# Gated mix of cached attention and a GeGLU feed-forward block, decode step: TensorE's work of 31 tiles as a hardware loop, values in one buffer, keys in two, semaphores by hand

## The chip, the core and the metric

The kernel runs on one NeuronCore of a Trainium2 chip. The core has five engines that run their own instruction streams and meet at semaphores: TensorE (PE in the profile; its weight loads are listed apart as PEld), VectorE (DVE), ScalarE (ACT), GpSimd (POOL) and SyncE (SP). Here SP issues all transfers; they run on 16 DMA engines, which read device memory (HBM) and write the core's working memory, SBUF. Matrix products land in a second, smaller memory, PSUM. The metric is the device time of one execution in microseconds; the kernel before took 1314.42 us (median of three runs, 1314.0 to 1314.48).

## What is computed

```python
x = A_x                                                  # 4 x 1 x 512
g = sigmoid((x * gate_w).sum(-1, keepdims=True))
q = (x @ wq) -> 4 x 32 heads x 1 x 128
scores = einsum("bhqd,bhkd->bhqk", q, k_cache) * 128 ** -0.5     # 4096 keys per head
o = einsum("bhqk,bhkd->bhqd", softmax(scores), v_cache)
a = o -> 4 x 1 x 4096 @ wo
b = (gelu(x @ w_gate) * (x @ w_up)) @ w_down             # 512 -> 1792 -> 512
out = g * a + (1 - g) * b
```

Everything is float32. The two caches, 4 x 32 x 4096 x 128 each, are 268 MB apiece; the weights together are 27.8 MB. Each cache element is used once.

## The kernel before

The batch of 4 and the 32 heads are cut into NT = 32 tiles: tile i takes batch row b = i % 4 and four heads of group g = i // 4. The keys of a tile are one SBUF tile of 128 partitions x 16384 floats (8.39 MB, 64 KB to a partition): 32 partitions per head, each with R = 128 consecutive keys of 128 numbers. The values of a tile have the same layout.

SBUF has room for three such tiles (pool `kv`, three buffers in rotation). Every large load takes the next buffer, in the order in which SP issues it: wq, then keys and values of tile 0, keys and values of tile 1 and so on, before the last values the two feed-forward weights `w_gate` and `w_up` together, and after them `w_down` with 18 of wo's 32 rows per partition, and the remaining 14 rows in five pieces. `load_next` (L105) issues one load. A load into a buffer waits until the last reader of what lies there is done, so in the steady state values i+1 go where keys i lay, and keys i+2 where values i lay.

For a tile i the work is this:

- `multiply(i)` (L195): DVE multiplies the keys by the query, which `spread` has laid out for four batch rows at once in `QB`. The last RP = 20 of the 128 keys of each partition are multiplied into PSUM (`big`, L198), the first 108 in place in SBUF (L199).
- `add_up(i)` (L201): DVE sums the 108 products of SBUF (L202) and then the 20 of PSUM (L203) over the 128 numbers; this gives `SC`.
- `weights(i)` (L205): the largest score of each head (DVE, L208 to L212), then four exponentials with row sums on ACT (L215), one for each head, into `PM` and `RS`.
- `values(i)` (L224): 32 float32 matmuls with `PM` as weights and the values as moving operand, 512 columns each, into four column groups of one PSUM bank, `po`. Each is two passes in the profile, 64 records to a tile.
- `gather(i)` (L232): ACT copies `po` to `o`, a matmul with `wide` folds it into the rows of batch row b of `g`.
- Every fourth tile: `totals` (L220, sums over the partitions), `turn` (L240, turns the group's result), `divide` (L248, DVE, into `OT`) and `spread` (L184, the next group's queries).

The order is written out by hand in the loop of L281 to L300: `values(i-1)` and its gathering stand behind `multiply(i)`. Semaphores are put in by the framework. All instructions of all tiles stand one after another in each engine's stream.

In the last round `ffn_up` (L253) runs on PE before `add_up(31)`, and `gelu` on DVE and ACT after it. The tail from L304 projects the hidden layer and the attention output with `down`, turns `OT` into `OW`, adds wo's last rows as their pieces land (L342 to L350), and stores the result (L353).

## Time and profile before

| what | value |
|---|---|
| median of three runs | 1314.42 us |
| the profiled execution, its own time | 1313.86 us |
| the profiled execution, span on the core | 1312.1 us |
| DVE busy | 1141.9 us (87%) |
| PE busy | 381.7 us (29%) |
| ACT busy | 106.9 us (8%) |
| bytes moved by DMA | 565.07 MB, mean 431 GB/s |

The profile is one execution. Its span runs from the first to the last instruction on the core; the execution's own time has 1.76 us more around it. L12 is line 12 of the kernel before. A row of the groups gives busy time and mean duration, and behind the second bar the idle time of the engine just before these instructions, with what ended most of it. Rows of the timeline give the start in us, the duration, the engine, the line, the operation, and in brackets how long the engine had been idle and what released it; "SPq" is SP issuing a transfer. Rows of a window give the stretch in us, its length, the busy time of each engine with its instructions, the granted TensorE clock, the DMA engines' mean busy share and GB/s; packets count where they start, so that a share over a short stretch can exceed 1.

### The profile page before, as it was taken

How to read it: one execution, taken by the hardware profiler on the slowest of the kernel's cores; microseconds unless marked ns; L12 is line 12 of the kernel's file. 1: busy time of each engine (PE TensorE's matmuls, PEld its weight loads, DVE VectorE, ACT ScalarE, POOL GpSimd, SP SyncE). 2: the span in 40 equal slices, each digit the busy share in tenths (PEclk: the TensorE clock that was granted, in tenths of full speed). 3: DMA queues.
4: the chain of work that ended last, by engine and by line, in shares of the span. 5: the costliest groups of instructions: out<-in, count | busy, mean ns of one | idle time of the engine just before them, and what ended most of it. 6: DMA issues, size and time to landing. Idle time of an engine off the chain costs nothing.

```text
span 1312.1 us, 6178 instructions
## 1 busy us (share of the span) xinstructions
PE 381.7 (29%) x2590; PEld 99.6 (8%) x2590; DVE 1141.9 (87%) x280; ACT 106.9 (8%) x344; POOL 0.7 (0%) x6
## 2 busy tenths in 40 slices
PE   2132113333212233221333321233332123332147
PEld 0000001000000001000010000000010000100012
DVE  1788899988899988988989888998889898898891
ACT  0000010001000010000000001000110001000001
POOL 0000000000000000000000000000000000000000
PEclk9666566666566666656666656666665566666579
DMA  9999999999999999999999999999999999999998
GB/s 416 440 424 446 418 442 422 442 432 438 434 430 436 432 434 440 434 430 434 430 440 432 438 430 434 430 436 438 432 440 424 440 428 438 442 424 442 420 421 351
DMA packets 10863, 565.07 MB, mean 431 GB/s; under 512 B 1212, under 2 KB 1228, under 8 KB 1620
## 3 DMA queue, kind: packets, MB, share of 16 engines
q1 hardware_dynamic: 10836, 564.69, 99.5%
q8 instruction: 20, 0.33, 0.1%
q14 instruction: 7, 0.06, 0.0%
HBM read 564.67 MB, written 0.01 MB: 430 GB/s over the span
## 4 chain that ended last, share of the span: by engine, by line
DVE 42%; DMA 41%; PE 12%; ACT 3%; issue 2%; SPq 0%; DVEq 0%; ACTq 0%
DMA kv<-in_A_k_cache 38%; DVE SC L202 18%; DVE kv L199 18%; PE po L229 11%; DVE SC L203 3%; ACT PM L215 3%; DVE big L198 2%; DMA kv<-in_A_wo 2%; DMA o<-in_A_x 2%; DVE m L208 0%; PE po L168 0%; PE big L168 0%; PE sm L221 0%; DVE mt L210 0%; DVE nm L212 0%
## 5 line engine op out<-in xcount | busy, mean ns | idle before, releaser
L229 PE MATMUL po<-kv,PM 128*16 128x512 f32 x2048 | 293.7, 738 | 664.9 <-ACT PM L215 664.9
L202 DVE TENSOR_REDUCE SC<-kv 128x108 f32<-128x13824 f32 x32 | 465.7, 14553 | 3.2
L199 DVE TENSOR_TENSOR kv<-kv,QB 128x13824 f32<-128x13824 f32 x32 | 465.6, 14551 | 0.0
L198 DVE TENSOR_TENSOR big<-kv,QB 128x2560 f32<-128x2560 f32 x32 | 90.7, 2833 | 103.9 <-DMA kv<-in_A_k_cache 103.9
L215 ACT ACTIVATE PM<-SC,nm 32x128 f32<-32x128 f32 x128 | 65.9, 515 | 775.7 <-DVE nm L212 749.2
L229 PEld LDWEIGHTS po<-kv,PM 128*16 128x16 f32 x2048 | 61.8, 113 | 882.6 <-ACT PM L215 679.9
L203 DVE TENSOR_REDUCE SC<-big 128x20 f32<-128x2560 f32 x32 | 90.1, 2815 | 0.0
L221 PE MATMUL sm<-RS,ones 128*128 128x16 f32 x16 | 4.9, 385 | 200.7 <-ACT PM L215 200.7
L235 ACT ACTIVATE o<-po 128x512 f32<-128x512 f32 x32 | 19.1, 597 | 303.5 <-PE po L229 303.5
L238 PE MATMUL g<-o,wide 128*64 128x512 f32 x64 | 34.3, 618 | 24.3 <-ACT o L235 24.3
L215 ACT ACTIVATION_READ_ACCUMULATOR PM<-SC,nm 32x1 f32 x128 | 24.9, 195 | 0.0
L221 PEld LDWEIGHTS sm<-RS,ones 128*128 128x128 f32 x16 | 4.0, 311 | 202.8 <-ACT PM L215 202.8
L142 DVE COPY xT<-sm 128x32 f32<-128x32 f32 x4 | 0.5, 184 | 21.1 <-PE sm L140 21.1
L250 DVE RECIPROCAL ri<-sm 128x16 f32<-128x16 f32 x8 | 2.0, 249 | 10.0 <-PE sm L246 10.0
L238 PEld LDWEIGHTS g<-o,wide 128*64 128x64 f32 x64 | 6.1, 134 | 53.8 <-ACT o L235 53.8
L208 DVE TENSOR_REDUCE m<-SC 128x1 f32<-128x128 f32 x32 | 9.2, 286 | 1.1
L246 PE MATMUL sm<-ident,gs 64*128 64x16 f32 x64 | 8.5, 262 | 4.8 <-ACT gs L242 4.8
L178 DVE COPY QT<-big 128x16 f32<-128x16 f32 x8 | 0.9, 180 | 10.1 <-PE big L176 10.1
L352 DVE COPY res<-g 128x128 f32<-128x128 f32 x1 | 0.3, 292 | 10.5 <-PE g L349 10.5
L189 PE MATMUL po<-ident,QX 128*128 128x128 f32 x64 | 9.2, 286 | 0.0
L260 PE MATMUL po<-kv,xT 128*32 128x448 f32 x64 | 8.1, 661 | 3.5 <-DMA kv<-in_B_w_up 3.5
L190 ACT ACTIVATE QB<-po 128x512 f32<-128x512 f32 x8 | 4.8, 597 | 52.1 <-DVE kv L199 51.4
(65 smaller groups left out, 95.7 us busy)
## 6 DMA issues: line engine op xcount, KB each, us to landing
kv<-in_B_w_gate SPq DMA_DIRECT2D x1, 3584.0 KB
kv<-in_B_w_up SPq DMA_DIRECT2D x1, 3584.0 KB, 23.3
kv<-in_B_w_down SPq DMA_DIRECT2D x1, 3584.0 KB
kv<-in_A_wo SPq DMA_DIRECT2D x1, 2560.0 KB, 18.6
kv<-in_A_wo SPq DMA_DIRECT2D x1, 2048.0 KB, 23.0
kv<-in_A_wo SPq DMA_DIRECT2D x2, 1024.0 KB, 17.2
kv<-in_A_wo SPq DMA_DIRECT2D x1, 768.0 KB
kv<-in_A_k_cache SPq DMA_DIRECT2D x32, 30.5
```

The costliest lines, as they stand in the source:

```text
L189: nc.tensor.matmul(t[:, b, :], QX[:, b].rearrange("p h k -> p (h k)"), ident, start=True, stop=True)
L198: nc.vector.tensor_tensor(big, k[:, R1:], q.to_broadcast([P, RP, D]), op=OP.mult)
L199: nc.vector.tensor_tensor(k[:, :R1], k[:, :R1], q.to_broadcast([P, R1, D]), op=OP.mult)
L202: nc.vector.tensor_reduce(SC[:, :R1], keys(i)[:, :R1], axis=AX.X, op=OP.add)
L203: nc.vector.tensor_reduce(SC[:, R1:], big, axis=AX.X, op=OP.add)
L208: nc.vector.tensor_reduce(m1, SC, axis=AX.X, op=OP.max)
L215: nc.scalar.activation(PM[s, :, h], SC[s, :], AF.Exp, bias=nm[s, :], scale=1.0, accum_out=RS[s, b, h:h + 1])
L221: nc.tensor.matmul(tot.rearrange("p b h -> p (b h)"), ones, RS.rearrange("p b h -> p (b h)"), start=True, stop=True)
L229: nc.tensor.matmul(po[32 * c:32 * c + M], p[:, j * M:(j + 1) * M], T["v", i][:, j * RJ * D:(j + 1) * RJ * D], start=j < 4, stop=j >= n - 4)
L235: nc.scalar.activation(o, po, AF.Copy)
L238: nc.tensor.matmul(G[g], wide[:, (3 - b) * M:(7 - b) * M], o, start=b == 0, stop=b == B - 1)
L246: nc.tensor.matmul(quo, gs[:, j, :], pick[:, :, j, :], start=j == 0, stop=j == RJ - 1)
```

## The change

The whole kernel body stands in one critical section in which the framework adds no semaphores. `Line` keeps, for each engine, the number of marked instructions and what it has already waited for.

- Values always lie in one buffer, `V`; keys alternate between two, `K[0]` and `K[1]`. wq is loaded into `V` first, then keys 0 and 1; values 0 follow when PE is done with wq. In the loop SP issues keys i+2 when the scores of tile i are summed, then values i+1 when `values(i)` is done. So values i+1 stand behind keys i+2 in the queue, where before they stood ahead of them.
- DVE multiplies all 128 keys of a partition in place in one instruction and sums them in one; `big`, the PSUM tile of products, is gone.
- PE's work of tiles 0 to 30 is one hardware loop on PE alone (`nc.tensor.Fori`): the query of the next tile (one matmul instead of four every fourth tile), the totals, the 32 value matmuls, and the turning (four matmuls), now done for each tile. The gathering matmul and the copy of `g` are gone; DVE divides for each tile. Inside the loop PE waits on counters that it lowers again (`token_a`, `token_d`, `sem_v`).
- The feed-forward weights go into `K[0]` after the scores of tile 30 and ahead of values 31, `w_down` and the first of wo into `K[1]` after the scores of tile 31, the last of wo into `K[0]` after the hidden layer is done. Feed-forward work on PE follows the loop and comes ahead of tile 31's values.
- At the end SP issues the store, GpSimd clears the semaphores, and SP waits for the store.

```diff
+class Line:
+
+
+    def __init__(self, engine, sem):
+        self.engine, self.sem, self.n, self.seen = engine, sem, 0, {}
+
+    def do(self, instruction):
+        instruction.then_inc(self.sem, 1)
+        self.n += 1
+        return self.sem, self.n
+
+    def wait(self, *marks):
+        for sem, n in marks:
+            if self.seen.get(id(sem), 0) < n:
+                self.engine.wait_ge(sem, n)
+                self.seen[id(sem)] = n
...
+    K = [kv.tile([P, TW], F32, name=f"k{s}") for s in range(2)]
+    V = kv.tile([P, TW], F32, name="v")
...
-    T = {}
-
-    def place(key):
-        T[key] = kv.tile([P, TW], F32, name="kv")
-        return T[key]
...
-    def load_kv(kind, i):
-        nc.sync.dma_start(place((kind, i)), heads(kc if kind == "k" else vc, i))
...
-    for i in range(NT):
-        LOADS.append(lambda i=i: load_kv("k", i))
-        if i == NT - 1:
-            LOADS.append(load_ffn_up)
-        LOADS.append(lambda i=i: load_kv("v", i))
-    LOADS += [load_down, load_last]
-    LOADS = iter(LOADS)
-
...
+    def load(dst, src, sem=None, name=None):
+        sem = sem or semaphore(name)
+        nc.sync.dma_start(dst, src).then_inc(sem, 16)
+        return sem, 16
+
+    def load_k(i):
+        load(K[i % 2], heads(kc, i), sem_k[i % 2])
+
+    def load_v(i):
+        load(V, heads(vc, i), sem_v)
+
+    got_q = load(V, wq.rearrange("(p c) n -> p (c n)", c=KC), name="got_q")
+    x_sb = o[:B]
+    got_x = load(x_sb, x.rearrange("b s d -> (b s) d"), name="got_x")
+    gw = gs[:B]
+    got_g = load(gw, gate_w.rearrange("(o n) -> o n", o=1).to_broadcast([B, DM]), name="got_g")
+    load_k(0)
+    load_k(1)
...
-    def multiply(i):
-        k = keys(i)
-        q = QB[:, i % B, None, :]
-        nc.vector.tensor_tensor(big, k[:, R1:], q.to_broadcast([P, RP, D]), op=OP.mult)
-        nc.vector.tensor_tensor(k[:, :R1], k[:, :R1], q.to_broadcast([P, R1, D]), op=OP.mult)
-
-    def add_up(i):
-        nc.vector.tensor_reduce(SC[:, :R1], keys(i)[:, :R1], axis=AX.X, op=OP.add)
-        nc.vector.tensor_reduce(SC[:, R1:], big, axis=AX.X, op=OP.add)
...
+    def spread_query(i):
+        g, b = divmod(i, B)
+        return nc.scalar.activation(QX, QT[:, b, HT * g:HT * g + HT, None].to_broadcast([P, HT, PH]), AF.Copy)
+
+    def spread():
+        return nc.tensor.matmul(qp[:, :D], QX.rearrange("p h k -> p (h k)"), ident, start=True, stop=True)
+
+    def take_query(i):
+        return AC.do(nc.scalar.activation(QB[i % 2], qp[:, :D], AF.Copy, scale=scale))
+
+    def totals():
+        return nc.tensor.matmul(tot, ones, RS, start=True, stop=True)
+
+    def values():
         p = PM.rearrange("p r h -> p (r h)")
         n = R // RJ
         for j in range(n):
             c = j % 4
-            nc.tensor.matmul(po[32 * c:32 * c + M], p[:, j * M:(j + 1) * M],
-                             T["v", i][:, j * RJ * D:(j + 1) * RJ * D], start=j < 4, stop=j >= n - 4)
-
...
+    def turn():
+        for j in range(RJ):
+            t = nc.tensor.matmul(quo, o[:, j * D:(j + 1) * D], pick[:, j, :], start=j == 0, stop=j == RJ - 1)
...
+    at_spread = [(PE.sem, PE.n + 3 * i + 1) for i in range(L1)]
+    at_values = [(PE.sem, PE.n + 3 * i + 2) for i in range(L1)]
+    at_turn = [(PE.sem, PE.n + 3 * i + 3) for i in range(L1)]
+    with nc.tensor.Fori(0, L1):
+        spread().then_inc(PE.sem, 1)
+        nc.tensor.wait_ge(token_a, 2).then_inc(token_a, -2)
+        nc.tensor.wait_ge(token_d, 1).then_inc(token_d, -1)
+        totals()
+        nc.tensor.wait_ge(sem_v, 16).then_inc(sem_v, -16)
+        values().then_inc(PE.sem, 1)
+        nc.tensor.wait_ge(token_a, 1).then_inc(token_a, -1)
+        turn().then_inc(PE.sem, 1)
+    PE.n += 3 * L1
+
+    summed, have_nm, have_OT = {}, {}, {}
...
+    def keys(i):
+        k = K[i % 2].rearrange("p (r d) -> p r d", d=D)
+        DV.wait((sem_k[i % 2], 16 * (i // 2 + 1)), have_QB[i])
+        DV.wait(DV.do(nc.vector.tensor_tensor(k, k, QB[i % 2][:, None, :].to_broadcast([P, R, D]), op=OP.mult)))
+        sc = SC[i % 2]
+        summed[i] = DV.do(nc.vector.tensor_reduce(sc, k, axis=AX.X, op=OP.add))
+        DV.wait(summed[i])
+        DV.wait(DV.do(nc.vector.tensor_reduce(m1, sc, axis=AX.X, op=OP.max)))
+        DV.wait(DV.do(nc.vector.transpose(mt, m1.to_broadcast([P, 32]))))
+        have_nm[i] = DV.do(nc.vector.tensor_reduce(NM[i % 2], mt, axis=AX.X, op=OP.max, negate=True))
+
...
+    def divide(i, at):
         g, b = divmod(i, B)
...
+        DV.wait(at)
+        DV.wait(DV.do(nc.vector.reciprocal(ri, tot)))
+        return nc.vector.tensor_tensor(OT[:, b, HT * g:HT * g + HT], quo, ri, op=OP.mult)
...
+    def weights(i):
+        AC.wait(have_nm[i])
+        if i:
+            AC.wait(at_values[i - 1])
+        for h in range(HT):
+            s = slice(h * PH, (h + 1) * PH)
+            t = nc.scalar.activation(PM[s, :, h], SC[i % 2][s, :], AF.Exp, bias=NM[i % 2][s, :], scale=1.0,
+                                     accum_out=RS[s, h:h + 1])
+        return t
+
+    SP.wait(wq_done)
+    load_v(0)
+    for i in range(NT):
+        keys(i)
+        if i > 0:
+            divide(i - 1, at_turn[i - 1]).then_inc(token_d, 1)
+        if i < L1:
+            AC.wait(at_spread[i])
+            have_QB[i + 1] = take_query(i + 1)
+            if i + 2 < NT:
+                spread_query(i + 2).then_inc(token_a, 1)
+            else:
+                nc.scalar.sem_inc(token_a, 1)
+            weights(i).then_inc(token_a, 1)
+            AC.wait(at_values[i])
+            nc.scalar.activation(o, po, AF.Copy).then_inc(token_a, 1)
+        if i + 2 < NT:
+            SP.wait(summed[i])
+            load_k(i + 2)
+        if i + 1 < L1:
+            SP.wait(at_values[i])
+            load_v(i + 1)
+    have_PM = AC.do(weights(L1))
+
+    f, down = K[0], K[1]
+    wo_rows = wo.rearrange("(p i) n -> p (i n)", i=WR)
+    SP.wait(summed[NT - 2])
+    got_up = [load(f[:, s * KC * F:(s + 1) * KC * F], a.rearrange("(p c) n -> p (c n)", c=KC), name=f"got_up{s}")
+              for s, a in enumerate((w_gate, w_up))]
+    SP.wait(at_values[L1 - 1])
+    load_v(L1)
+    SP.wait(summed[L1])
+    got_down = load(down[:, :DR * DM], w_down.rearrange("(p i) n -> p (i n)", i=DR), name="got_down")
+    got_wo = [load(down[:, (DR + r0) * DM:(DR + r1) * DM], wo_rows[:, r0 * DM:r1 * DM], name=f"got_wo{r0}")
+              for r0, r1 in ((0, W0), (W0, W1))]
...
-    for i in range(NT):
-        g, b = divmod(i, B)
-        multiply(i)
-        if i > 0:
-            if b == 0:
-                totals(g - 1)
-            values(i - 1)
-            gather(i - 1)
-            load_next()
-        if b == 0 and i > 0:
-            turn(g - 1)
-        if b == B - 1 and i < NT - 1:
-            spread(g + 1)
...
+    SP.wait(have_hT)
+    got_w = []
+    r0 = 0
+    for n in PIECES:
+        got_w.append(load(f[:, r0 * DM:(r0 + n) * DM], wo_rows[:, (W1 + r0) * DM:(W1 + r0 + n) * DM],
+                          name=f"got_w{r0}"))
+        r0 += n
+
...
+    SP.wait(DV.do(nc.vector.tensor_copy(res, acc)))
+    load(out.rearrange("b s (c n) -> c (b s) n", c=4), res[::8], stored)
+    nc.sync.sem_inc(parting, 1)
+    nc.gpsimd.wait_ge(parting, 1).then_inc(parting, -1)
+    nc.gpsimd.sem_clear(range(counters[0].num, counters[-1].num + 1))
+    nc.sync.wait_ge(stored, 16).then_inc(stored, -16)
```

## The prediction, on record before the result

> **What bounds the kernel now.** I read the head of the page first, with the DMA queues.

> ```profile
> span 1312.1 us, 6178 instructions
> PE 381.7 (29%) x2590; PEld 99.6 (8%) x2590; DVE 1141.9 (87%) x280; ACT 106.9 (8%) x344; POOL 0.7 (0%) x6
> q1 hardware_dynamic: 10836, 564.69, 99.5%
> q8 instruction: 20, 0.33, 0.1%
> q14 instruction: 7, 0.06, 0.0%
> ```

> DVE at 87% looks like the busiest engine, but the data queue's packets fill 99.5% of 16 DMA engines' span. Every byte of caches and weights is still moved by the changed kernel, so the question is whether the transfers can be fed without holes, and what else uses the DMA engines. Next I cut the span into stretches (stretch, length, busy time of the engines, granted clock, DMA share, GB/s).

> ```profile
> 400.00:800.00 400.00, 110.05 (x706) 27.28 (x706) 365.41 (x76) 32.56 (x108) 0.00 (x0) 0.63 1.00 434
> 1200.00:1306.00 106.00, 51.28 (x416) 14.85 (x416) 77.39 (x33) 10.84 (x32) 0.00 (x0) 0.73 0.99 426
> 1275.00:1279.00 4.00, 0.00 (x0) 0.00 (x0) 3.93 (x4) 0.00 (x0) 0.00 (x0) 0.50 0.78 314
> ```

> The middle runs at a share of 1.00 and 434 GB/s: no hole to close. The last stage has one, 0.78 over 4 us, about 0.9 us for the average DMA engine. Then the timeline, for one tile, with its neighbours in the first and last tile.

> ```profile
> 42.30 2.83 DVE L198 TENSOR_TENSOR big<-kv,QB 128x2560 f32<-128x2560 f32 x1 [4.38 <-DMA kv<-in_A_k_cache]
> 80.81 2.83 DVE L198 TENSOR_TENSOR big<-kv,QB 128x2560 f32<-128x2560 f32 x1 [3.11 <-DMA kv<-in_A_k_cache]
> ...
> 622.27 9.30 PE L229 MATMUL po<-kv,PM 128*16 128x512 f32 x64 [26.92 <-ACT PM L215]
> 623.10 2.83 DVE L198 TENSOR_TENSOR big<-kv,QB 128x2560 f32<-128x2560 f32 x1 [3.13 <-DMA kv<-in_A_k_cache]
> 623.96 0.17 PEld L229 LDWEIGHTS po<-kv,PM 128*16 128x16 f32 x4 [0.68 <-issue]
> 624.81 0.17 PEld L229 LDWEIGHTS po<-kv,PM 128*16 128x16 f32 x4 [0.68 <-issue]
> 631.64 0.33 SPq L77 DMA_DIRECT2D kv<-in_A_k_cache  x1
> 655.08 0.33 SPq L77 DMA_DIRECT2D kv<-in_A_v_cache  x1
> 663.01 2.83 DVE L198 TENSOR_TENSOR big<-kv,QB 128x2560 f32<-128x2560 f32 x1 [4.44 <-DMA kv<-in_A_k_cache]
> ...
> 1243.90 2.83 DVE L198 TENSOR_TENSOR big<-kv,QB 128x2560 f32<-128x2560 f32 x1 [3.13 <-DMA kv<-in_A_k_cache]
> ```

> In all these rows DVE starts a tile when its keys land, after 3 to 4 us of idling: the transfers set the pace. From the first tile to the last, 31 tiles took 1243.90 - 42.30 = 1201.6 us, 38.76 each, and a tile's keys or values 19.38. The rows also give the lead, the time from a load's issue to the landing of the load ahead of it, when its own bytes can flow. Values issued at 655.08 follow keys that landed at 663.01: 7.9 us. Keys issued at 631.64 follow values that landed 19.4 after 623.1: 10.8 us. With these leads the share is 1.00.

> **The change part by part.** First DVE, by the groups (busy us, mean ns, idle before).

> ```profile
> L202 DVE TENSOR_REDUCE SC<-kv 128x108 f32<-128x13824 f32 x32 | 465.7, 14553 | 3.2
> L199 DVE TENSOR_TENSOR kv<-kv,QB 128x13824 f32<-128x13824 f32 x32 | 465.6, 14551 | 0.0
> L208 DVE TENSOR_REDUCE m<-SC 128x1 f32<-128x128 f32 x32 | 9.2, 286 | 1.1
> L250 DVE RECIPROCAL ri<-sm 128x16 f32<-128x16 f32 x8 | 2.0, 249 | 10.0 <-PE sm L246 10.0
> L251 DVE TENSOR_TENSOR OT<-sm,ri 128x16 f32<-128x16 f32 x8 | 1.4, 175 | 0.3
> ```

> Multiplying and summing all 16384 numbers in SBUF takes 14.55 x 16384 / 13824 = 17.25 us each, 34.5 together. Three small reductions, each at most L208's 0.29, and the division, now once a tile (0.25 + 0.18), add 1.3. That makes 35.8 us against 38.76 for the transfers. The 3.0 us between them cover it; DVE would have to lose all of them before the span grew. Dropping the products in PSUM is worth nothing by itself. It also takes away an early release: before, the key buffer was free after L202, ahead of the sums of `big`. Now it is free 34.5 us after the keys land.

> Keys i+2 may be issued then, and can flow when values i+1's predecessors are through: keys i land, values i, keys i+1 and values i+1 in the old order; now keys i, values i-1, keys i+1, values i, and then keys i+2. That is 3 x 19.38 = 58.1 us after keys i landed. The lead is 58.1 - 34.5 = 23.6 us, far over the 7.9 of before. Cost nothing; the price if the cover were gone is 1 us per tile and us.

> Values i+1 wait for `values(i)`, and this chain is the tighter one. Values i land, PE multiplies, SP issues. The rows from 622.27 to 631.64 show the same chain, 9.4 us. Its upper bound is a PE that stays slow: 0.85 us between the two loads of four weights at 623.96 and 624.81, and 16 such groups, 13.7 us. Values i+1 can flow after keys i+2, 19.38 after values i landed. The lead is 10.0 us, at worst 5.7. I take 10.0, since PE idles about as long ahead of it as before. That is again no shorter than the 7.9 that sufficed, so nothing.

> The query of keys i+2 now comes through PE's loop: values i land, 9.4 us of matmuls, a copy of `po`, four turning matmuls, the back edge, one `spread` matmul, a copy. The copies and matmuls have rows here:

> ```profile
> L235 ACT ACTIVATE o<-po 128x512 f32<-128x512 f32 x32 | 19.1, 597 | 303.5 <-PE po L229 303.5
> L246 PE MATMUL sm<-ident,gs 64*128 64x16 f32 x64 | 8.5, 262 | 4.8 <-ACT gs L242 4.8
> L238 PE MATMUL g<-o,wide 128*64 128x512 f32 x64 | 34.3, 618 | 24.3 <-ACT o L235 24.3
> L189 PE MATMUL po<-ident,QX 128*128 128x128 f32 x64 | 9.2, 286 | 0.0
> L221 PE MATMUL sm<-RS,ones 128*128 128x16 f32 x16 | 4.9, 385 | 200.7 <-ACT PM L215 200.7
> ```

> 0.6 for each copy, 2 x 0.3 for the two passes of `spread`, 8 x 0.26 for turning at most: 13.3 us, 6 us before keys i+2 land. A late query would delay only DVE, whose release of the buffer has 23.6 us to spare. On PE two gathering records per tile go, and turning, totals and spreading are done for every tile instead of every fourth; all of it lies in PE's idle time.

> Next the instruction fetch, which does lie on the bounding resource. 0.33 MB over PE's 5180 instructions is 64 bytes each, so q8 is PE's stream, in 20 pieces of 16 KB, 256 instructions. Its 0.1% of the span is 1.3 us on each of 16 engines, 0.7 to 2.0 by rounding. Of 2590 matmul records 2048 + 64 + 64 + 64 + 16 belong to tiles, and 334 stay. The loop body has 64 + 8 + 2 + 2 = 76 and stands once; tile 31 adds 74, the first query 2. That is 486, a fifth: 4 pieces for 20, if the loop's code is fetched once. 16/20 x 1.3 gives -1.05 us, between -0.5 and -1.6.

> The two ends:

> ```profile
> 0.74 0.39 SPq L110 DMA_DIRECT2D kv<-in_A_wq  x1
> ...
> 1261.11 4.91 PE L260 MATMUL po<-kv,xT 128*32 128x448 f32 x32 [3.52 <-DMA kv<-in_B_w_up]
> 1275.88 0.33 SPq L86 DMA_DIRECT2D kv<-in_B_w_down  x1
> 1286.26 21.62 DMA kv<-in_A_wo
> 1309.33 0.67 SPq L353 DMA_DIRECT2D out<-res  x1
> ```

> At the start keys 2 can be issued when tile 0 is summed, 42.30 + 34.5 = 76.9; values 0 take the place that keys 1 had in the queue, landing at 80.8. The lead is 3.9 us, the shortest of the changed kernel. Before, `w_down` had the like: issued at 1275.88, while the values ahead of it landed 19.4 after `w_up` (1261.1), at 1280.5: 4.6 us. That is the stretch at 0.78. Some of the 16 engines ran dry there while the last one, which sets a landing, was still at work. So 0 to 0.9 us; I take 0.2, as only the last engine counts. At the end `w_down` is now issued when tile 31 is summed, 34.5 us after its keys land instead of 32.0 (1243.90 to 1275.88), but these keys now stand ahead of values 30 and land 19.4 us earlier: a lead of 4.6 + 19.4 - 2.5 = 21.5 us. The last pieces of wo (chain of waits, 21.62 us of DMA from 1286.26) still arrive behind the same bytes, so the tail from there is unchanged. Entering the critical section ahead of the load at 0.74 and clearing semaphores behind 1309.33 are not in the trace; the store to the span's end took 2.8 us, and the clearing runs on POOL beside it. Nothing excludes a small gain; 0 to 1.4 us of loss for both (half of that 2.8), and I take 0.35, nearer to the cover.

> Sum: -1.05 + 0.2 + 0.35 = -0.5 us. The profiled execution took 1313.86 us (span 1312.1 and 1.76 around it), so 1313.4; the median of the runs, 1314.42, is 0.56 above it, so **1313.9 us**. The bounds give 1312.8 to 1316.2.

> **The rivals.** Within 0.2%, 2.6 us, this kernel can hardly be told from no change.

> The loop's code is fetched anew in each pass. The body (76 records and as many weight loads, 152, and its waits) is more than half of a piece, so that it more likely than not lies across two. Then 31 passes fetch 62 pieces and the rest about 4: 46 more than now at 0.065 us per engine, +3.0 instead of -1.05, 1317.9 us. With one piece a pass it is 15 more, +1.0, 1315.9. For it speaks that the 20 pieces of before come singly as PE moves on, so little is kept; against it, that no row shows what a jump back does. [...] Slower by more than 0.2% only in the two-piece form.

> The single value buffer holds up the transfers. The chain from landing to issue is 9.4 us and has 19.4, less what passes from an issue to its first packets.

> ```profile
> 1.00:1.50 0.50, 0.00 (x0) 0.00 (x0) 0.45 (x2) 0.50 (x1) 0.29 (x1) 1.00 0.00 0
> 1.50:2.00 0.50, 0.00 (x0) 0.00 (x0) 0.50 (x4) 0.50 (x1) 0.00 (x0) 1.00 4.69 1573
> ```

> The first load, issued at 0.74, has no packet before 1.50 and many by 2.00: about 1 us, so 18.4 are left. If PE, slow all through (13.7), also waits inside the matmuls for code that comes behind three packets of the data queue (0.995 x 16 x 1312.1 / 10836 = 1.9 us each, 5.8), the chain takes 19.5, and each us over 18.4 returns 31 times: 1.1 x 31 = +34 us, 1348 us. For it: values have no second buffer, and the loop's waits stand in PE's own stream. Against it: it takes two bad cases at once.

> The leads near the end help the last engine too. If the 0.99 of 1200 to 1306 and its 426 GB/s became the 434 of the middle, 106 x 8 / 434 = 2.0 us would go, 1311.9, and with the shorter code at its -1.6 bound 1311.4. For it: the hole at 1275. Against it: the late engines had no hole. [...]

> **How the numbers follow.** The forecast has 0.76, the refetch 0.10 (0.07 in two pieces), the value buffer 0.04, the gain at the end 0.10 (0.07 of it beyond 0.2%). Faster by over 0.2% gets 0.08, slower 0.07 + 0.04 and 0.02 from the forecast's own upper end, 0.13, and 0.79 remain. The range 1311.8 to 1317.9 takes in the refetch and most of the gain.

> **What would show it.** A DMA share of 1.00 in the middle and 38.7 to 38.8 us between the first multiplications; values issued some 10 us after they land, keys some 34.5; about 4 pieces on q8; DVE still waiting 2 to 3 us per tile for keys. More than 20 pieces on q8 would speak for the refetch; a share below 0.98 in the middle, or values as the releaser of SP's late issues, for the value buffer. A tile period off by 0.1 us is 3 us in all and would break the forecast.

## The result, and the profile after

The changed kernel took 1312.03 us (median of 20 runs, 1311.59 to 1312.92), the kernel before 1314.14 (20 runs beside them, 1313.73 to 1314.97). The ratio is 0.9985 with a 95% interval of 0.9978 to 0.9992: 2.1 us less, clear of no change, and less than 0.2%. The forecast was 1313.9, 0.5 less than the 1314.42 it started from.

The head of the changed kernel's page:

```profile
span 1310.7 us, 6525 instructions
PE 390.0 (30%) x2766; PEld 136.1 (10%) x2766; DVE 1142.5 (87%) x263; ACT 108.7 (8%) x360; POOL 0.7 (0%) x6
...
q1 hardware_dynamic: 10836, 564.69, 99.5%
q8 instruction: 4, 0.07, 0.0%
q14 instruction: 6, 0.05, 0.0%
```

The data queue still fills 99.5% of the span. PE executes more instructions than before (2766 matmul records for 2590), but its code comes in 4 pieces instead of 20.

The timeline of the changed kernel (start, duration, engine, line; L269 is the multiplication, L231 the values' matmuls, L127 the issue of a load), for the first tile, two in the middle, and the last stage:

```profile
0.96 0.39 SPq L127 DMA_DIRECT2D v<-in_A_wq  x1
42.58 17.22 DVE L269 TENSOR_TENSOR k<-k,QB 128x16384 f32<-128x16384 f32 x1 [3.70 <-DMA k<-in_A_k_cache]
77.08 0.33 SPq L127 DMA_DIRECT2D k<-in_A_k_cache  x1
...
604.65 17.22 DVE L269 TENSOR_TENSOR k<-k,QB 128x16384 f32<-128x16384 f32 x1 [3.13 <-DMA k<-in_A_k_cache]
621.91 17.22 DVE L271 TENSOR_REDUCE SC<-k 128x128 f32<-128x16384 f32 x1
624.09 9.42 PE L231 MATMUL bank<-v,PM 128*16 128x512 f32 x64 [19.84 <-PEq L258]
633.56 0.33 SPq L127 DMA_DIRECT2D v<-in_A_v_cache  x1
634.31 1.03 PE L237 MATMUL bank<-pick,o 128*128 128x4 f32 x8 [0.81 <-PEq L260]
635.19 0.47 PE L218 MATMUL bank<-ident,QX 128*128 128x128 f32 x2
635.70 0.28 ACT L221 ACTIVATE QB<-bank 128x128 f32<-128x128 f32 x1 [1.53 <-PE bank L218]
639.16 0.33 SPq L127 DMA_DIRECT2D k<-in_A_k_cache  x1
643.24 17.23 DVE L269 TENSOR_TENSOR k<-k,QB 128x16384 f32<-128x16384 f32 x1 [3.04 <-DMA k<-in_A_k_cache]
...
1257.36 0.33 SPq L127 DMA_DIRECT2D k<-in_B_w_down  x1
1259.09 4.91 PE L338 MATMUL bank<-k,xT 128*32 128x448 f32 x32 [2.60 <-DMA k<-in_B_w_up]
1278.46 9.90 PE L231 MATMUL bank<-v,PM 128*16 128x512 f32 x64 [14.15 <-DMA v<-in_A_v_cache]
1307.71 0.67 SPq L127 DMA_DIRECT2D out<-res  x1
```

With the same points of the kernel before the spans divide as follows. The same bytes stand ahead of `w_up`'s landing in both.

| stretch | before | after | difference |
|---|---|---|---|
| start to the first multiplication | 42.30 | 42.58 | +0.28 |
| from there to `w_up`'s landing (first matmul on it) | 1261.11 - 42.30 = 1218.81 | 1259.09 - 42.58 = 1216.51 | -2.30 |
| from there to the issue of the store | 48.22 | 48.62 | +0.40 |
| from there to the end of the span | 2.77 | 2.99 | +0.22 |
| span | 1312.1 | 1310.7 | -1.4 |

So the gain arose in the middle, and the ends gave some of it back. The profiled executions themselves took 1313.86 and 1312.45 us; the changed one is 0.4 above its median, which is why the spans show 1.4 us and the medians 2.1. The stretches of the changed kernel, as before with DMA share and GB/s last:

```profile
400.00:800.00 400.00, 114.47 (x788) 40.56 (x780) 364.24 (x77) 35.74 (x121) 0.00 (x0) 0.62 1.00 434
1200.00:1306.00 106.00, 54.22 (x458) 18.04 (x462) 60.94 (x29) 8.51 (x24) 0.00 (x0) 0.71 0.98 423
```

The middle reads 1.00 and 434 GB/s in both kernels. A gain of 0.2% in it is not to be seen in these columns; only the starts of the tiles show it.

### The profile page after: what moved, and what is told of

The parts are those of the page before. It is cut to its first block, busy times and chain, and to the rows that moved or that the text cites. A ratio compares the mean times of both kernels' runs of the same rounds, so it can differ in the third digit from the quotient of the medians.

```text
span 1310.7 us, 6525 instructions
## 1 busy us (share of the span) xinstructions
PE 390.0 (30%) x2766; PEld 136.1 (10%) x2766; DVE 1142.5 (87%) x263; ACT 108.7 (8%) x360; POOL 0.7 (0%) x6
## 3 DMA queue, kind: packets, MB, share of 16 engines
q1 hardware_dynamic: 10836, 564.69, 99.5%
## 4 chain that ended last, share of the span: by engine, by line
DMA 51%; DVE 48%; PE 1%; issue 0%; SPq 0%; ACT 0%
DMA k<-in_A_k_cache 45%; DVE k L269 24%; DVE SC L271 24%; DMA k<-in_B_w_up 3%; DMA k<-in_A_wo 3%; PE bank L338 0%; PE bank L428 0%; SPq L127 0%; DVE m L273 0%; DVE k L354 0%; DVE mt L274 0%; DVE k L351 0%; DVE k L352 0%; DVE nm L275 0%; ACT k L349 0%
## 5 line engine op out<-in xcount | busy, mean ns | idle before, releaser
L269 DVE TENSOR_TENSOR k<-k,QB 128x16384 f32<-128x16384 f32 x32 | 551.2, 17225 | 82.6 <-DMA k<-in_A_k_cache 82.6
L271 DVE TENSOR_REDUCE SC<-k 128x128 f32<-128x16384 f32 x32 | 551.0, 17220 | 1.1
L231 PE MATMUL bank<-v,PM 128*16 128x512 f32 x2048 | 294.7, 740 | 569.8 <-PEq L258 555.7
L231 PEld LDWEIGHTS bank<-v,PM 128*16 128x16 f32 x2048 | 69.4, 113 | 768.5 <-issue 754.3
L224 PE MATMUL bank<-RS,ones 128*128 128x4 f32 x64 | 17.7, 347 | 288.0 <-PEq L256 288.0
L308 ACT ACTIVATE o<-bank 128x512 f32<-128x512 f32 x31 | 18.5, 597 | 869.2 <-PE bank L231 869.2
L224 PEld LDWEIGHTS bank<-RS,ones 128*128 128x128 f32 x64 | 15.8, 306 | 294.3 <-issue 294.3
L237 PE MATMUL bank<-pick,o 128*128 128x4 f32 x256 | 32.9, 252 | 25.1 <-PEq L260 25.1
L237 PEld LDWEIGHTS bank<-pick,o 128*128 128x128 f32 x256 | 31.0, 191 | 53.6 <-issue 52.7
L167 DVE COPY xT<-bank 128x32 f32<-128x32 f32 x4 | 0.5, 182 | 21.5 <-PE bank L163 21.5
L218 PE MATMUL bank<-ident,QX 128*128 128x128 f32 x64 | 15.0, 316 | 1.5 <-ACT QX L215 1.5
L221 ACT ACTIVATE QB<-bank 128x128 f32<-128x128 f32 x32 | 8.9, 278 | 47.3 <-PE bank L218 47.3
L215 ACT ACTIVATE QX<-QT 128x128 f32<-128x128 f32 x32 | 9.9, 308 | 2.4 <-DVE QT L209 1.6
```

The lines of the kernel that those rows point to most:

```text
L215: return nc.scalar.activation(QX, QT[:, b, HT * g:HT * g + HT, None].to_broadcast([P, HT, PH]), AF.Copy)
L218: return nc.tensor.matmul(qp[:, :D], QX.rearrange("p h k -> p (h k)"), ident, start=True, stop=True)
L221: return AC.do(nc.scalar.activation(QB[i % 2], qp[:, :D], AF.Copy, scale=scale))
L224: return nc.tensor.matmul(tot, ones, RS, start=True, stop=True)
L231: t = nc.tensor.matmul(po[32 * c:32 * c + M], p[:, j * M:(j + 1) * M], V[:, j * RJ * D:(j + 1) * RJ * D], start=j < 4, stop=j >= n - 4)
L237: t = nc.tensor.matmul(quo, o[:, j * D:(j + 1) * D], pick[:, j, :], start=j == 0, stop=j == RJ - 1)
```

## Experiments

Two theories stood against each other. The code theory: fetching PE's code delays single DMA engines, and since the last of the 16 sets each landing (the changed kernel's keys have 16 landings from 640.8 to 643.2 us, and the multiplication on them starts at 643.24), this costs more than its mean share. The lead theory: the longer leads of the loads, and no products in PSUM, brought the gain.

**The changed kernel again.**

> The changed kernel once more, beside the other three on one chip. 1312.0 us, 2.1 below the kernel before, with 4 code pieces on q8.

1312.28 us (1311.42 to 1313.05, 11 runs; 0.9983 of before, 0.9974 to 0.9992), 3 pieces. With the 20 runs above the median of 31 is 1312.1.

**The loop written out.** PE executes the same instructions in the same order; they only stand 31 times.

```diff
-    with nc.tensor.Fori(0, L1):
+    for _ in range(L1):
```

> The changed kernel with PE's loop written out 31 times; all else stays. Code theory (fetching PE's code delays single DMA engines, and the last engine sets each landing): about 20 pieces on q8, keys every 38.7 to 38.8 us, and the 2.3 us of the middle come back: 1314.1 to 1314.5 us. My predicted size for the code alone was 1.05: 1313.1. Lead theory (longer leads of the loads and no products in PSUM brought the gain): it stays at 1312.0 to 1312.4.

1314.35 us (1314.16 to 1314.94; ratio 1.0000, 0.9991 to 1.0009): the whole gain is gone. Its queue of code pieces, and the same two points as above:

```profile
q8 instruction: 22, 0.36, 0.1%
```

```profile
42.19 17.23 DVE L269 TENSOR_TENSOR k<-k,QB 128x16384 f32<-128x16384 f32 x1 [4.28 <-DMA k<-in_A_k_cache]
...
1261.83 4.91 PE L338 MATMUL bank<-k,xT 128*32 128x448 f32 x32 [3.06 <-DMA k<-in_B_w_up]
```

The middle takes 1219.64 us, 0.8 more than in the kernel before and 3.1 more than with the loop. Buffers, order of loads, semaphores and the products in SBUF are those of the changed kernel here, and they bring nothing measurable. The lead theory falls: the gain hangs on the code being written out or not.

**Twice the code.** 39 unused matmuls per tile, in the time in which PE waits for the values:

```diff
         totals()
+        for _ in range(39):
+            nc.tensor.matmul(bank[4][:, :P], ones, ident, start=True, stop=True)
         nc.tensor.wait_ge(sem_v, 16).then_inc(sem_v, -16)
```

> The loop written out as before, with 39 more matmuls per tile (their result is used by nothing) ahead of PE's wait for the values, so that PE's code doubles while PE would idle. Code theory: about 40 pieces on q8 and another 2 to 3 us on top of the loop written out, 1316 to 1317.5 us. Lead theory: no change against the loop written out, within 0.5 us.

1318.21 us (1317.97 to 1319.64; ratio 1.0031, 1.0019 to 1.0043), 41 pieces: 3.9 us for 19 more pieces, more than the 2 to 3 expected. Its last stretches say how the delay comes about:

```profile
1304.00:1306.00 2.00, 1.57 (x16) 0.22 (x8) 0.00 (x0) 0.37 (x1) 0.00 (x0) 1.00 1.00 418
1306.00:1308.00 2.00, 1.30 (x40) 1.06 (x40) 0.00 (x0) 0.23 (x1) 0.00 (x0) 1.00 0.68 281
1308.00:1310.00 2.00, 1.08 (x32) 0.81 (x32) 0.00 (x0) 0.00 (x0) 0.00 (x0) 1.00 0.50 209
1310.00:1312.00 2.00, 1.17 (x36) 0.90 (x40) 0.00 (x0) 0.00 (x0) 0.00 (x0) 1.00 0.46 180
1312.00:1314.00 2.00, 0.74 (x22) 0.23 (x12) 0.29 (x1) 0.00 (x0) 0.00 (x0) 1.00 0.00 0
```

and the last stretches of the changed kernel:

```profile
1302.00:1304.00 2.00, 1.08 (x32) 0.81 (x32) 0.00 (x0) 0.00 (x0) 0.00 (x0) 1.00 0.96 388
1304.00:1306.00 2.00, 1.44 (x28) 1.14 (x32) 0.00 (x0) 0.00 (x0) 0.00 (x0) 0.68 0.27 109
1306.00:1308.00 2.00, 1.32 (x24) 0.80 (x19) 0.29 (x1) 0.00 (x0) 0.00 (x0) 0.50 0.03 9
```

With the doubled code the share stands at one half for some five microseconds before it drops to nothing: half of the engines are through, the other half are still moving data. With the loop it drops in two. The trace has 16 landings for each load, read here as one from each engine. Those of the last piece of wo, in us of the span:

```
kernel before        1306.0 1306.0 1306.1 1306.1 1306.1 1306.3 1306.3 1306.7 1306.7 1306.8 1307.0 1307.1 1308.1 1308.2 1308.2 1308.5
changed kernel       1304.0 1304.1 1304.1 1304.2 1304.2 1304.3 1304.3 1304.4 1304.4 1304.4 1304.7 1305.5 1305.9 1305.9 1306.2 1306.4
loop written out     1304.5 1304.6 1304.6 1304.7 1305.0 1305.1 1306.3 1306.5 1307.3 1307.4 1308.0 1308.8 1308.9 1308.9 1309.0 1309.0
twice the code       1306.8 1306.9 1307.0 1307.0 1307.0 1307.2 1307.2 1307.5 1311.7 1312.0 1312.0 1312.1 1312.1 1312.2 1312.2 1312.3
```

Twice the code splits the engines into eight that end near 1307.1 and eight near 1312.1, 5.0 us apart.

The landings of the earlier loads show how the lag, the time from the first of the 16 landings to the last, comes about. With twice the code it jumps five times, from one load to the next: 0.7 to 2.2, 1.8 to 3.1, 3.2 to 4.5, 4.7 to 6.0 and 6.1 to 7.4 us, each time at the load during which piece 1, 9, 17, 25 or 33 is fetched (at 85.4, 319.1, 571.7, 826.6 and 1081.6). With the loop written out it jumps at pieces 1, 9 and 17 (0.5 to 1.7, 1.9 to 3.0, 3.4 to 4.4), and so it does in the kernel before (0.8 to 1.7, 1.8 to 3.0, 3.2 to 4.4); the changed kernel has the first jump alone (0.8 to 2.6). Read from these jumps, eight pieces apart, and from the eight and eight landings above, the pieces go to eight engines in turn. A packet of code takes 0.88 to 0.97 us in the kernel before, and the jumps are mostly 1.1 to 1.5 us; in this reading only every eighth piece falls on the engine that is already last. At the landing of `w_up` this adds up to:

| landing of `w_up`, us | kernel before | changed kernel | loop written out | twice the code |
|---|---|---|---|---|
| first of the 16 | 1256.5 | 1256.6 | 1257.1 | 1257.7 |
| last of the 16 | 1261.0 | 1259.1 | 1261.8 | 1264.7 |
| lag | 4.5 | 2.4 | 4.7 | 7.0 |

PE's first matmul on `w_up` starts at 1261.11 in the kernel before, behind the last landing. The first engines lie within 1.2 us of one another, and the lag makes most of the differences: the code theory holds. With twice the code the 7.0 us shrink to 5.5 by the end. There the first landing of the last values comes 21.1 us after that of `w_up`, and 19.3 in the changed kernel; read here, the engines ahead ran dry in between.

**The same matmuls in the loop.** PE works as much as in the last kernel, from code that stands once.

```diff
     with nc.tensor.Fori(0, L1):
...
         totals()
+        for _ in range(39):
+            nc.tensor.matmul(bank[4][:, :P], ones, ident, start=True, stop=True)
```

> The changed kernel with its loop, and in it the same 39 more matmuls per tile (their result is used by nothing) as in the doubled code: PE works as much, but its code stands once. Code theory: 4 to 6 pieces on q8 and the time of the changed kernel, 1312.0 to 1312.6 us. Rival (PE's extra work, not its code, cost the 3.9 us): 1315 to 1316 us.

1313.07 us (1311.88 to 1314.76; 0.9988, 0.9979 to 0.9997), 4 pieces. That is 0.8 above the changed kernel's 1312.28, slightly over the expected band, and 5.1 below the doubled code: about a fifth of the 3.9 us, at most, is PE's extra work.

**A body of over three pieces.** Five tiles to a pass.

```diff
-    with nc.tensor.Fori(0, L1):
-        spread().then_inc(PE.sem, 1)
+    with nc.tensor.Fori(0, 6):
+        for _ in range(5):
+            spread().then_inc(PE.sem, 1)
...
+    for _ in range(1):
+        spread().then_inc(PE.sem, 1)
```

> The changed kernel with five tiles in each pass of the loop (6 passes, and one tile after them): a body of about 840 instructions, over three pieces of 256. If PE keeps only two pieces, each pass fetches its body anew, 20 to 25 pieces on q8 and the time of the loop written out, 1314.0 to 1314.6 us. If PE keeps the whole body, 6 or 7 pieces and 1312.0 to 1312.6 us.

1311.78 us (1311.53 to 1312.32; 0.998, 0.9971 to 0.9989), and on q8:

```profile
q8 instruction: 7, 0.11, 0.0%
```

Six passes over a body of about 840 instructions (an estimate: five times the 152 matmuls and weight loads that a tile has in the trace, and its waits) fetch 7 pieces in all, so the body is kept. That PE keeps only two pieces was a supposition, and up to this size the 7 pieces refute it. Seven pieces cost no more than four (1311.78 us, against 1312.03 and 1312.28), as the turn of eight, read above, has it.

**Products in PSUM.** The loop kept, 16 keys' products in four PSUM banks that the loop leaves free:

```diff
+            DV.do(nc.vector.tensor_tensor(inner, k[:, R1:], q.to_broadcast([P, 16, D]), op=OP.mult))
+            DV.wait(DV.do(nc.vector.tensor_tensor(k[:, :R1], k[:, :R1], q.to_broadcast([P, R1, D]), op=OP.mult)))
+            summed[i] = DV.do(nc.vector.tensor_reduce(sc[:, :R1], k[:, :R1], axis=AX.X, op=OP.add))
+            DV.wait(DV.do(nc.vector.tensor_reduce(sc[:, R1:], inner, axis=AX.X, op=OP.add)))
```

> The changed kernel, loop and all, with the products of the last 16 keys of each partition in PSUM (tiles 0 to 30), and the keys' buffer released when the other 112 are summed. Code theory: as the changed kernel, within 0.4 us, 1312.0. Lead theory, as far as the products in PSUM are its cause: up to 2 us slower, 1314.

1312.82 us (1312.08 to 1313.4; 0.9986, 0.9977 to 0.9995), against 1312.28 for the changed kernel on the same chip: no difference that these intervals can tell.

**No products in PSUM in the kernel before.**

```diff
-        nc.vector.tensor_tensor(big, k[:, R1:], q.to_broadcast([P, RP, D]), op=OP.mult)
-        nc.vector.tensor_tensor(k[:, :R1], k[:, :R1], q.to_broadcast([P, R1, D]), op=OP.mult)
+        nc.vector.tensor_tensor(k, k, q.to_broadcast([P, R, D]), op=OP.mult)
...
-        nc.vector.tensor_reduce(SC[:, :R1], keys(i)[:, :R1], axis=AX.X, op=OP.add)
-        nc.vector.tensor_reduce(SC[:, R1:], big, axis=AX.X, op=OP.add)
+        nc.vector.tensor_reduce(SC, keys(i), axis=AX.X, op=OP.add)
```

> The kernel before with all products in SBUF, multiplied in one instruction and summed in one: the key buffer is free 34.5 us after the keys land instead of 32.0, so that the lead of the next values falls from 7.9 to about 4.5 us. My reading (a lead over some 1 to 2 us costs the last engine nothing): 1314.1 us, within 0.4. Lead theory: slower, by up to 0.1 us per tile, 1317 us.

1331.7 us (1329.05 to 1334.2; 1.013, 1.0114 to 1.0145): 17.5 us slower, and my reading of the lead is refuted. Its timeline and one of its stretches:

```profile
627.12 0.33 SPq L77 DMA_DIRECT2D kv<-in_A_v_cache  x1
632.50 17.22 DVE L198 TENSOR_TENSOR kv<-kv,QB 128x16384 f32<-128x16384 f32 x1 [4.62 <-DMA kv<-in_A_k_cache]
...
667.08 0.33 SPq L77 DMA_DIRECT2D kv<-in_A_v_cache  x1
671.18 17.22 DVE L198 TENSOR_TENSOR kv<-kv,QB 128x16384 f32<-128x16384 f32 x1 [3.35 <-DMA kv<-in_A_k_cache]
```

```profile
400.00:800.00 400.00, 109.09 (x721) 26.52 (x714) 357.78 (x55) 32.33 (x107) 0.00 (x0) 0.63 0.99 424
```

Leads of 5.4 and 4.1 us instead of 7.9, and 424 GB/s instead of 434, while the share falls by 0.01 only. So the PSUM tile of the kernel before earned its place by the release: the next values were issued 655.08 - 623.10 = 32.0 us after the multiplication began, and here 667.08 - 632.50 = 34.6. These 2.6 us held the transfers together. The changed order of loads does without it.

**Late values.** The changed kernel with a short lead for the values of tiles 10 to 30:

```diff
+        if 10 <= i < L1:
+            SP.wait(at_values[i - 1], summed[i])
+            load_v(i)
         if i + 2 < NT:
             SP.wait(summed[i])
             load_k(i + 2)
-        if i + 1 < L1:
+        if i + 1 < 10:
             SP.wait(at_values[i])
             load_v(i + 1)
```

> The changed kernel with the load of values 10 to 30 issued only when the scores of the same tile are summed, about 15 us after the values before landed instead of 9.5: their lead falls from 10 to about 4 us. My reading: as the changed kernel, within 0.5 us, 1312.0 to 1312.5. Lead theory: engines that run ahead run dry each tile, 0.3 us or more per tile, over 1318 us.

1316.89 us, with runs from 1313.13 to 1319.26 (1.0017, 1.0006 to 1.0028): 4.8 us above the changed kernel, between the two expectations, 0.2 us per tile. The lead was 604.48 - 600.42 = 4.1 us:

```profile
600.42 0.33 SPq L127 DMA_DIRECT2D v<-in_A_v_cache  x1
600.79 0.43 SPq L127 DMA_DIRECT2D k<-in_A_k_cache  x1
604.48 17.23 DVE L269 TENSOR_TENSOR k<-k,QB 128x16384 f32<-128x16384 f32 x1 [3.05 <-DMA k<-in_A_k_cache]
```

**Late values with more code.** If an engine that runs ahead has to wait for the last one at every short lead, the delays of different engines should add up instead of passing side by side. The same edit on the loop written out:

> The loop written out (about 22 code pieces) and values 10 to 30 issued late (their lead about 4 us), both together. Theory of added delays (with a short lead an engine that runs ahead runs dry and waits for the last, so that the delay of every code piece counts in full, whichever engine it falls on; with a long lead only the sum on one engine counts): the 15 or so pieces of tiles 10 to 30 at 0.9 to 1.4 us each count singly, less the 2 us that they cost already: 1326 to 1336 us. Rival (a short lead costs so much per tile, whatever the code): 1314.4 and the 4.7 us that late values cost with the loop, 1319 us.

1320.11 us (1318.55 to 1322.27; 1.0044, 1.003 to 1.0058): near the rival. As the runs with late values scatter, both were run once more on another chip, and twice the code with late values beside them.

> Late values with the loop once more, on the same chip as the doubled code with late values. Its runs spread over 6 us before: 1313 to 1319, median 1317.

> Late values with the loop written out once more, on the same chip. If delays add up: more than 4 us above late values with the loop. If not: 2.1 us above it, as with long leads.

> The doubled code (about 41 pieces) and values 10 to 30 issued late. If delays add up under a short lead: about 27 pieces of those tiles at 0.5 us or more each on top of the doubled code's 1318.2, 1328 us or more. If a short lead costs the same whatever the code: 1318.2 + 4.7 = 1323 us.

1315.09 (1313.2 to 1317.5), 1321.33 (1318.31 to 1324.39) and 1325.32 us (1323.18 to 1327.62). The loop written out is now 6.2 us above the loop, which is over the 4 expected of delays that add up; twice the code lies between its two expectations. With both rounds together:

| code pieces on q8 | long leads | late values | difference |
|---|---|---|---|
| 3 or 4 (loop) | 1312.1 (31 runs) | 1315.9 (22) | 3.8 |
| 22 (written out) | 1314.35 (11) | 1320.8 (11) | 6.5 |
| 41 (twice the code) | 1318.2 (6) | 1325.3 (4) | 7.1 |

A short lead costs more where there is more code, from 3.8 to 6.5 us, but with 41 pieces hardly more than with 22. (The last round alone, on the chip on which the kernels with long leads had also run, gives 2.8, 7.0 and 7.1.) The landings fit: at `w_up` the lag is 1.1 and 1.2 us in the two profiles of late values with the loop, and 1.5 and 2.1 in those with the loop written out, instead of 2.4 and 4.7 with long leads; read here, the engines ahead have waited for the last. Delays adding up explain the first step and not the second; what puts the engines out of step in the kernel with 4 pieces stays open.

## Why the prediction was right, and where its steps were off

The time lay in the range and the sign was right, but that the range held is in part luck. The sum's own bounds were 1312.8 to 1316.2, and 1312.03 lies below them; the range reached down to 1311.8 only because it took in most of a gain at the end, and that gain did not come. The terms of the sum, one by one:

- **The instruction fetch** was the right mechanism, and the term that was mis-sized: -1.05 us, bounds -0.5 to -1.6. Measured, the loop written out costs 1314.35 - 1312.28 = 2.1 us more than the loop. The step that failed is "0.1% of the span is 1.3 us on each of 16 engines", 0.065 us a piece. It spread the pieces evenly over all engines, though the prediction itself says for the start that only the last engine counts. As read from the landings, the pieces go to eight engines in turn, and the 20 of the kernel before delay the last engine three times (pieces 1, 9 and 17: 0.9, 1.2 and 1.2 us); the loop takes away two of the three delays, the two of 1.2 us. As a mean per piece that is 2.07 / 19 = 0.11 us between the loop and the code written out, and 3.86 / 19 = 0.20 up to the doubled code, 0.16 if the 0.8 us of PE's extra work are taken off.
- **DVE**: 17.25 us for each instruction was forecast; 17.22 was measured. From tile 7 on it still waits for the keys 3.0 to 3.1 us per tile, against 2 to 3 expected. Tiles 1 to 5 follow one another without that wait (the second starts at 77.76, the third at 113.22), since keys 0 and 1 now land one behind the other.
- **The leads** came as worked out. Values are issued 633.56 - 624.09 = 9.5 us after their predecessors are in use (9.4 forecast), 9.7 us ahead of the keys' landing at 643.24 (10.0). Keys are issued 34.5 us after landing, as forecast. `w_down` leads by 1278.46 - 1257.36 = 21.1 us (21.5). The query is ready 11.9 us after the values' first matmul (13.3).
- **What a lead is worth** was wrong, though it did not touch the sum. The prediction put the limit at about 1 us, "so 18.4 are left" of 19.4. The kernel before without PSUM and the late values show that 4 to 5 us already cost 0.2 to 0.6 us per tile (17.5 / 31 at the upper end), while 7.9 and 10 cost nothing: the loop written out, with leads of 10 and 23, is no faster than the kernel before with 7.9 and 10.8. For the value buffer's rival this means less room than was said: the chain took 9.5 us and had some 11 to 14 (19.4 less a lead of 5 to 8), not 18. That code waits behind three packets of data, as that rival supposed, no run shows; the values' matmuls took 8.34 to 9.98 us in the changed kernel's 31 passes, not 13.7.
- **Keys 2 at the start**: 0.2 us was taken. None is to be seen: the load was issued at 77.08 as worked out (76.9), and the stretch from 2 to 100 us moved 437 GB/s (430 before).
- **The ends**: 0.35 us was forecast, and +0.28 and +0.22 were found at the first multiplication and behind the store. "The tail from there is unchanged" was not quite so, at +0.40.

The refetch did not come: 4 pieces on q8 with 31 passes, and 7 with six passes over a body of five tiles, which spans more than three pieces. That pieces come singly as PE moves on, from which the prediction took that "little is kept", does not say what is kept: all of five tiles is. How much more PE could keep, no run here shows. The gain at the end did not come either: `w_down` now leads by 21 us, and the last stage still reads 0.98 and 423 GB/s, which fits a hole that only engines ahead of the others had: behind it the lag of the kernel before is 2.4 us, and 4.5 ahead of it.

## What to carry to other kernels

Here the transfers bound the kernel (q1 fills 99.5% of the span), and its time followed the DMA engine that ended last: at `w_up` the first of the 16 landings differ by 1.2 us between four kernels and the last by 5.6. What used a few of the engines (code of a long, written-out stream) was to be priced on those few, not as a mean share over sixteen: one piece in eight counted, at 1.1 to 1.5 us. A hardware loop on the engine with the most code (PE, 5180 of 6178 instructions) took 20 pieces down to 4 and two of the three jumps away. And the lead of each load, from its issue to the landing of the one ahead, is worth reading before a release is moved: here 8 us were enough and 4 to 5 were not, while the DMA share still read 0.99 to 1.00.

## What the runs showed of the hardware that was not expected

- The back edge of PE's loop is not to be seen: from the start of the turning matmuls to the first matmul of the next pass it is 635.19 - 634.31 = 0.88 us. With the loop written out it is 0.89:

```profile
635.80 1.03 PE L237 MATMUL bank<-pick,o 128*128 128x4 f32 x8 [0.81 <-PEq L260]
636.69 0.47 PE L218 MATMUL bank<-ident,QX 128*128 128x128 f32 x2
```
